# A common issue order for the second batch's attention beside the first batch's mixer, with its levels in single pieces

## The chip, the cores and the metric

One NeuronCore of a Trainium2 chip runs the whole kernel. The metric is the device time of one execution in microseconds (us); lower is better. In this kernel TensorE multiplies matrices (7,828 matmuls in the profile), VectorE (729 instructions) and ScalarE (452) do elementwise work, GpSimd (46) sets masks, and SyncE issues most of the transfers. "Granted clock" is a column of the profile, the share of TensorE's full clock that was granted; the profile records its changes, and in the two profiles compared here its values are 1.00 and 0.50.

## The reference

```python
# r, k, v, w: (4 batches, 8 heads, 768 tokens, 48); u: (8, 48); all float32
for t in range(S):                                   # attention with a running state
    cur = einsum('bhd,bhe->bhde', u[None] * k_t, v_t)
    y[:, :, t] = einsum('bhd,bhde->bhe', r_t, state + cur)
    state = w_t[..., None] * state + einsum('bhd,bhe->bhde', k_t, v_t)
x = y.transpose(0, 2, 1, 3).reshape(4, 768, 384)
h = maximum(x.T_tokens @ w_tok1, 0) @ w_tok2         # mixes tokens (256 hidden)
z = x + h.T
out = z + maximum(z @ w_ch1, 0) @ w_ch2              # mixes channels (1536 hidden)
```

The mixer's weights arrive as 64-bit floats and are turned into 32-bit floats on the chip, in pairs of blocks, by six VectorE instructions and one ScalarE instruction a pair.

## The kernel before

Attention is done in twelve units of 256 tokens, three units a batch. Inside a unit six levels (l = 0 to 5) combine ever larger blocks of tokens (the units of the third and fourth batch combine two levels at a time): each level has a product of keys and queries (`gram`), an in-place scaling of both (`join`) and a copy of the wanted part of the product (`pick`). The first product takes special copies of the queries and keys, `rp` and `kp`, which ScalarE makes. Then the keys are transposed (`tokens`, copied to `kT`), the state's increments are computed (`carry`, to `kv_ps`), the state is advanced (`update`), and the output is the sum of two products (`before` from the state, `within` from the levels) in `y_ps`. One PSUM buffer serves `kv_ps` and `y_ps` in turn.

While one batch's mixer runs, the next batch's attention runs beside it. Two lists of pieces with weights are merged by their share of the total:

```python
def woven(*lists):
    keyed = []
    for n, pieces in enumerate(lists):
        total, at = sum(c for c, _ in pieces), 0.0
        for i, (c, f) in enumerate(pieces):
            keyed.append(((at + c / 2) / total, n, i, c, f))
            at += c
    return [(c, f) for *_, c, f in sorted(keyed, key=lambda e: e[:3])]

def strict(*fs):                  # each engine keeps the order of emission
    for f in fs:
        done = len(block.instructions)
        f()
        for ins in block.instructions[done:]:
            if ins.engine in in_turn:
                tc.add_manual_dep(ins, in_turn[ins.engine], no_sync, reason="order of issue")
                in_turn[ins.engine] = ins.name
```

Outside `strict`, the scheduler of the compiler chooses the order of each engine's instructions. In the kernel before, the stage of the first batch's mixer and the second batch's attention is free in this way; later stages are strict:

```python
        def block(l):
            gram(l); join(l, products[l], products[l + 1]); pick(l)   # one piece of the list
# ... in beside(i, after, ahead), for the second batch's units:
            return [(1.0, begin[1]), tokens, one(carry, rest[0]), update, one(before, rest[1]), one(within, rest[2]),
                    *loads[:2], *rest[3:], ...]
# ... in quarters(s), seven products with ten or so VectorE additions around them:
            if bt == 0:
                return [(0.01, begin)] + [(1.96, p) for p in (p1, p4, p2, p5, p6, p7, p3)]
# ... in the loop over batches:
            if bt == 0:
                emit(woven(att, pieces))                              # free
            else:
                if bt == 1:
                    in_turn = {e.engine: newest(e) for e in (pe, dve, act)}
                strict(*(f for _, f in woven(att, pieces)))
```

## Time and profile before

| | kernel before |
|---|---|
| time, median | 589.5 us (588.8 to 590.2), profiled execution 593.75 |
| span of the profiled execution | 591.4 us |
| TensorE, VectorE, ScalarE busy | 95%, 66%, 30% |
| first stretch (conversions), 94.3 to 127.9 | 33.6 us |
| first mixer + second attention, 127.9 to 226.4 ("the stage") | 98.5 us |
| from there to the end | 365.0 us |

The stage is taken here from the first product of `h_ps` of the channel mixer (line 652) to the first product of the next batch's token mixer (line 615). This is the view of busy time by windows: start and end, length, then busy us and count of TensorE, TensorE's weight loads, VectorE, ScalarE and GpSimd, then granted clock, share of the DMA engines and GB/s.

### The profile page before, as it was taken

The numbers are of one execution on the slowest core, as the hardware profiler recorded it, in microseconds if no ns is written. First come the engines' busy times: TensorE is split into PE (matmuls) and PEld (weight loads), VectorE is DVE, ScalarE is ACT, GpSimd is POOL, SyncE is SP. The second block draws the span as 40 slices with busy tenths as digits, with TensorE's granted clock in tenths as the row PEclk, the third lists the DMA queues.
The fourth block names the chain that finished last, engine by engine and source line by source line (L and its number), as shares of the span: only waits on it lengthen the run. The fifth ranks groups of instructions, "written<-read, shape, count | busy, mean of one in ns | idle before, by whom it ended". The sixth has DMA issues, their size and how long they took to land.

```text
span 591.4 us, 17486 instructions
## 1 busy us (share of the span) xinstructions
PE 562.9 (95%) x7828; PEld 484.6 (82%) x7828; DVE 392.0 (66%) x729; ACT 179.5 (30%) x452; POOL 9.6 (2%) x46
## 2 busy tenths in 40 slices
PE   3779989999999989999999999999999999999997
PEld 2668757876898876789899896889898886898987
DVE  5779699999785696687878775768866232040313
ACT  6144535432414422332323303332313212302020
POOL 4000000000100000000000000000000000000000
PEclk9999999999999999999999999999999999999999
DMA  8526465612224224123232022011010000000000
GB/s 333 211 63 166 133 210 180 200 47 80 76 84 109 71 68 149 28 55 86 77 109 89 23 94 68 1 55 50 7 55 29 1 28 1 0 28 1 27 1 27
DMA packets 23017, 46.13 MB, mean 78 GB/s; under 512 B 2464, under 2 KB 14880, under 8 KB 22944
## 3 DMA queue, kind: packets, MB, share of 16 engines
q1 hardware_dynamic: 22800, 45.03, 24.4%
q8 instruction: 61, 1.00, 0.7%
q14 instruction: 12, 0.10, 0.1%
q10 hardware_dynamic: 144, 0.00, 0.0%
HBM read 40.31 MB, written 4.72 MB: 76 GB/s over the span
## 4 chain that ended last, share of the span: by engine, by line
PE 78%; DVE 13%; issue 3%; DMA 3%; ACT 2%; SPq 0%; DVEq 0%; ACTq 0%
PE z_ps L642 27%; PE q_ps L676 23%; PE gram L308 4%; PE h_ps L622 4%; PE h_ps L615 4%; PE gram L386 3%; PE kv_ps L524 2%; PE y_ps L576 2%; PE h_ps L652 2%; PE gram L513 2%; DVE rk L342 2%; PE y_ps L563 2%; DVE scratch L218 2%; DVE scratch L215 1%; PE gram L302 1%
## 5 line engine op out<-in xcount | busy, mean ns | idle before, releaser
L642 PE MATMUL z_ps<-xT,wch 128*128 128x256 f32 x864 | 194.4, 381 | 1.6 <-ACT z L644 1.6
L642 PEld LDWEIGHTS z_ps<-xT,wch 128*128 128x128 f32 x864 | 161.5, 190 | 24.4 <-ACT z L644 2.6
L644 ACT ACTIVATE z<-z_ps 128x256 f32<-128x256 f32 x144 | 55.0, 383 | 178.0 <-PE z_ps L642 177.9
L676 PE MATMUL q_ps<-wch,z 128*128 128x192 f32 x528 | 93.4, 328 | 0.0
L676 PEld LDWEIGHTS q_ps<-wch,z 128*128 128x128 f32 x528 | 86.5, 190 | 1.3
L676 PE MATMUL q_ps<-scratch,z 128*128 128x192 f32 x396 | 69.6, 328 | 0.0
L676 PEld LDWEIGHTS q_ps<-scratch,z 128*128 128x128 f32 x396 | 64.8, 190 | 0.7 <-issue 0.3
L308 PEld LDWEIGHTS gram<-rk 48*64 48x64 f32 x1536 | 35.3, 177 | 8.9 <-issue 4.0
L308 PE MATMUL gram<-rk 48*64 48x32 f32 x1536 | 37.7, 256 | 5.0 <-issue 2.6
L720 DVE TENSOR_TENSOR z<-z 128x768 f32<-128x768 f32 x9 | 8.6, 954 | 47.4 <-ACT z L644 47.4
L342 DVE TENSOR_TENSOR rk<-rk,decay 112x1024 f32<-112x1024 f32 x24 | 29.4, 1224 | 15.3 <-PE gram L302 9.8
L412 DVE COPY_PREDICATED at<-mask,gram 128x384 f32<-128x384 uint8 (+2 forms) x72 | 34.5, 482 | 1.4
L622 PE MATMUL h_ps<-h,wtok 128*128 128x384 f32 x96 | 35.0, 491 | 0.0
L615 PE MATMUL h_ps<-x,wtok 128*128 128x384 f32 x96 | 34.0, 507 | 0.0
L342 DVE TENSOR_TENSOR rk<-rk,w 112x1024 f32<-112x1024 f32 x24 | 29.3, 1223 | 6.5 <-PE gram L308 6.1
L624 DVE TENSOR_TENSOR x<-x,h_ps 128x384 f32<-128x384 f32 x24 | 13.2, 551 | 30.5 <-PE h_ps L622 30.5
L615 PEld LDWEIGHTS h_ps<-x,wtok 128*128 128x128 f32 x96 | 18.2, 195 | 11.1
L622 PEld LDWEIGHTS h_ps<-h,wtok 128*128 128x128 f32 x96 | 16.5, 190 | 9.8 <-ACT h L617 2.6
L580 ACT COPY x<-y_ps 128x384 f32<-128x384 f32 x12 | 5.8, 479 | 58.4 <-PE y_ps L576 58.4
L686 DVE TENSOR_TENSOR o<-x,z 128x192 f32<-128x192 f32 x11 | 3.9, 356 | 26.3 <-ACT z L685 26.2
L544 DVE TENSOR_TENSOR state<-state,kv_ps 128x192 f32<-128x192 f32 x40 | 14.1, 353 | 9.4 <-PE kv_ps L524 8.1
L285 PE MATMUL gram<-rp,kp 48*64 48x64 f32 x384 | 10.2, 270 | 10.3 <-ACT kp L273 8.1
(114 smaller groups left out, 658.3 us busy)
## 6 DMA issues: line engine op xcount, KB each, us to landing
rk<-in_rkw_dram SPq DMA_DIRECT2D x32, 192.0 KB, 3.7
vt<-in_v_dram SPq DMA_DIRECT2D x12, 384.0 KB, 3.8
out_dram<-o SPq DMA_DIRECT2D x24, 192.0 KB, 1.9
rp<-in_near_dram SPq DMA_DIRECT2D x12, 384.0 KB, 3.6
rk<-in_rkw_dram SPq DMA_DIRECT2D x8, 512.0 KB, 5.6
w<-in_rkw_dram SPq DMA_DIRECT2D x16, 192.0 KB, 3.6
x<-in_w_ch_dram SPq DMA_DIRECT2D x6, 512.0 KB, 4.7
rk<-in_w_ch_dram SPq DMA_DIRECT2D x6, 512.0 KB, 4.3
```

The lines of the kernel that those rows point to most:

```text
L218: dve.scalar_tensor_tensor(mf, mf, 2.0 ** -20, power.bitcast(bf16), op0=ALU.mult, op1=ALU.mult)
L308: fours(lambda q, j, rows, cols: pe.matmul(g[cols, q, ts(ca, 32)], k_[rows, ds(ca * 128 + j * T, T)], right[rows, ts(2 * ca + j, 32 // b), ...
L342: dve.tensor_mul(halves, halves, by)
L386: fours(lambda q, j, rows, cols: pe.matmul(g[cols, q, ts(a, 96)], k_[rows, ds((c * A + a) * 128 + j * T, T)], L["far", c][rows, ts(2 * a + ...
L412: dve.copy_predicated(out=to[:, :, :, (q + 1) * b:], data=got[:, :, :, first * b:first * b + n], mask=masks4[l][:, q].unsqueeze(1).unsquee ...
L544: dve.tensor_add(new, new, got)
L615: pe.matmul(sums[i], wtok1[:, c, ts(i, 128)], xs[bt][:, c, :], start=(c == 0), stop=(c == C - 1))
L622: pe.matmul(ps, wtok2[:, i, ts(c, 128)], h1[:, i, :], start=(i == 0), stop=(i == DTOK // 128 - 1))
L624: dve.tensor_add(x[:, c, :], x[:, c, :], ps)
L642: pe.matmul(ps, wch1[:, m, ts(jt, 128)], xT[:, m, ts(s, SEG)], start=(m == 0), stop=(m == DM // 128 - 1))
L644: act.activation(zs[s][:, jt, :], ps, AF.Relu)
L676: pe.matmul(ps, a[:, j, :], b[:, j, :], start=(j == 0), stop=(j == HJ - 1))
```

## The change

The intent was to give TensorE, VectorE and ScalarE one common order in this stage, as in the later ones, to split the levels into single pieces so that other work can stand between them, and to keep the conversion pairs from overtaking each other. The core of the diff (cuts marked):

```diff
     def whole(steps):
-        return (0.2, lambda: [f() for f in steps])
+        def all_steps():
+            mark = converted[-1]
+            for f in steps:
+                late(mark, dve, f)
+            converted.append(newest(dve))
+        return (0.2, all_steps)
...
+        if i >= UB:
+            pieces = [(0.1, begin), (1.9, lambda: join(0, ...)), (0.3, lambda: [gram0(c) for c in range(UC)]),
+                      *((0.7, lambda c=c: pick0(c)) for c in range(UC))]
+            for l in range(1, LEVELS):
+                pieces += [(0.3, gram l), (1.5, join l), (1.3 if l == 1 else 0.7, pick l)]
+            return pieces
...
-            if bt == 0:
-                return [(0.01, begin)] + [(1.96, p) for p in (p1, p4, p2, p5, p6, p7, p3)]
             return [(1.6, p1), (0.01, <sum s1>), (0.65, p4), ..., (0.3, p6), (1.0, p7), (1.6, p3)]
...
-            return [(1.0, begin[1]), tokens, one(carry, rest[0]), update, one(before, rest[1]), one(within, rest[2]),
-                    *loads[:2], *rest[3:], ...]
+            join0, gram0, pick0, pick1, *rest = rest
+            return [(0.3, tokens[1]), begin, join0, (0.3, both_of(carry, gram0)), loads[2], pick0, loads[3], pick1,
+                    (0.3, both_of(before, rest[0])), *rest[1:3], (0.3, both_of(within, rest[3])), *loads[:2], *rest[4:], ...]
...
-        total = sum(c for c, _ in pieces)              # units of the third and fourth batch
-        return [(c * 12 / total, f) for c, f in pieces]
...
-            if bt == 0:
-                emit(woven(att, pieces))
-            else:
-                if bt == 1:
-                    in_turn = {e.engine: newest(e) for e in (pe, dve, act)}
-                strict(*(f for _, f in woven(att, pieces)))
+            if bt == 0:
+                in_turn = {e.engine: newest(e) for e in (pe, dve, act)}
+            strict(*(f for _, f in woven(att, pieces)))
```

`loads[2]` and `loads[3]` are the two halves of the state update. No instruction is removed; orders change.

More of the change, by code (lines that the diff above doesn't have):

```diff
@@ L420, in levels @@
                 (1.5, join_r, (l,)), (1.5, pick4, (l, 0)), (1.5, pick4, (l, 1)))] + [(1.4, lambda: block(5))]
+        if i >= UB:
+            pieces = [(0.1, begin), (1.9, lambda: join(0, products[0], products[1])), (0.3, lambda: [gram0(c) for c in range(UC)]),
+                      *((0.7, lambda c=c: pick0(c)) for c in range(UC))]
+            for l in range(1, LEVELS):
+                pieces += [(0.3, lambda l=l: gram(l)), (1.5, lambda l=l: join(l, products[l], products[l + 1])),
+                           (1.3 if l == 1 else 0.7, lambda l=l: pick(l))]
+            return pieces
         for l in range(1, LEVELS):
@@ L665, in quarters @@
             L = {}
-            def begin():
-                dve.tensor_add(s1, a21, a22)
-                dve.tensor_sub(s2, s1, a11)
-                dve.tensor_sub(s4, a12, s2)
-                dve.tensor_sub(a21, a11, a21)
             def product(a, b):
@@ L741, in both, with both_of @@
                 tc.add_manual_dep(ins, behind, no_sync, reason="products in tiles together")
-        def one(*pieces):
-            return (sum(c for c, _ in pieces), lambda: both(*(f for _, f in pieces)))
+        def both_of(f, g):
+            return lambda: both(f[1], g[1])
         if i + 1 < NEAR:
-            return [(1.0, begin[1]), tokens, one(carry, rest[0]), update, one(before, rest[1]), one(within, rest[2]),
-                    *loads[:2], *rest[3:], *([(0.0, begin_near)] if i == NEAR - 2 else [])]
+            join0, gram0, pick0, pick1, *rest = rest
+            return [(0.3, tokens[1]), begin, join0, (0.3, both_of(carry, gram0)), loads[2], pick0, loads[3], pick1,
+                    (0.3, both_of(before, rest[0])), *rest[1:3], (0.3, both_of(within, rest[3])), *loads[:2], *rest[4:],
+                    *([(0.0, begin_near)] if i == NEAR - 2 else [])]
         far0, far1, copies, gram, join_k, join_r, pick0, pick1 = rest[:8]
@@ L754, in visit @@
         def visit(f, g):
-            return (0.3, lambda: both(f[1], g[1]))
-        pieces = [*nearest(i), (0.3, tokens[1]), (1.9, begin[1]), far0, far1, (1.0, copies[1]), visit(carry, gram), join_k, join_r, loads[2],
+            return (0.3, both_of(f, g))
+        return [*nearest(i), (0.3, tokens[1]), (1.9, begin[1]), far0, far1, (1.0, copies[1]), visit(carry, gram), join_k, join_r, loads[2],
                   later0, pick0, loads[3], later1, copies_, pick1, visit(before, gram_), join_k_, join_r_, (0.01, lambda: load_near(i + 1)),
                   pick0_, pick1_, visit(within, last), *loads[:2]]
-        total = sum(c for c, _ in pieces)
-        return [(c * 12 / total, f) for c, f in pieces]
     hiddens, turned, ups, downs = mixing(0)
@@ L791, in rwkv6_then_mixer @@
         if bt == 0:
+            converted = [in_turn[dve.engine]]
             to_ch = [whole(e[n < 2:]) for n, e in enumerate(to_ch)]
@@ L797, in rwkv6_then_mixer @@
             weight_sums()
-            converted = newest(dve)
+            summed = newest(dve)
             load_rkw(UB + 2)
@@ L812, in rwkv6_then_mixer @@
             if bt == 0:
-                begin, first, *rest = levels(n)
-                att = [begin, (first[0], lambda f=first[1]: late(in_turn[dve.engine], dve, lambda: late(
-                    in_turn[pe.engine], pe, f)))] + [(c, lambda f=f: late(converted, dve, f)) for c, f in rest]
+                begin, join0, *rest = levels(n)
+                att = [begin, join0] + [(c, lambda f=f: late(summed, dve, f)) for c, f in rest]
             for i in range(n, n + UB):
```

## The prediction

> **What bounds the kernel now.** I first read the busy time by stage (window start and end, length, then busy us and instruction count of each engine), because TensorE's 95% over the span hides stages of different kinds.
>
> ```profile
> 94.30:128.00 33.70, 32.13 (x150) 27.50 (x149) 31.93 (x40) 16.62 (x32) 0.00 (x0) 1.00 0.51 157
> 139.60:154.00 14.40, 14.31 (x410) 11.18 (x411) 13.08 (x20) 5.42 (x15) 0.00 (x0) 1.00 0.09 31
> 154.00:173.00 19.00, 18.98 (x520) 17.62 (x510) 15.36 (x28) 6.00 (x15) 2.50 (x15) 1.00 0.35 96
> 173.00:202.00 29.00, 28.64 (x751) 24.37 (x744) 17.98 (x33) 11.25 (x30) 0.11 (x1) 1.00 0.32 85
> 202.00:226.50 24.50, 22.64 (x524) 20.85 (x522) 23.02 (x59) 6.41 (x19) 0.11 (x1) 1.00 0.34 92
> 226.50:356.00 129.50, 129.50 (x1678) 113.55 (x1678) 96.29 (x204) 36.48 (x101) 0.23 (x2) 1.00 0.25 75
> ```
>
> From 139.6 to 226.5 the mixer of batch 0 runs beside the attention of batch 1: this is the stage the change reorders. TensorE idles there only 2.3 us (differences of the first two columns), and from 226.5 on not at all. So whatever the stage gains or loses, the end gains or loses. VectorE is nearly full in its first and last windows.
>
> Then the timeline, for the waits a new order can lengthen.
>
> ```profile
> 140.81 0.66 ACT L269 COPY kp<-rk 112x512 f32<-112x512 f32 x1 [12.35 <-PE gram L285]
> 141.37 1.31 ACT L273 ACTIVATE kp<-rk,u_col 112x128 f32<-112x128 f32 x4
> 142.58 0.67 ACT L269 COPY rp<-rk 112x512 f32<-112x512 f32 x1
> 142.71 1.23 DVE L342 TENSOR_TENSOR rk<-rk,w 112x1024 f32<-112x1024 f32 x1
> 143.14 1.32 ACT L273 ACTIVATE rp<-rk,u_col 112x128 f32<-112x128 f32 x4
> ...
> 160.38 0.67 ACT L269 COPY kp<-rk 112x512 f32<-112x512 f32 x1 [2.33 <-issue]
> 160.96 1.31 ACT L273 ACTIVATE kp<-rk,u_col 112x128 f32<-112x128 f32 x4
> ...
> 183.98 1.13 PE L285 MATMUL gram<-rp,kp 48*64 48x64 f32 x64
> ```
>
> ScalarE makes kp and rp in 1.87 us each (140.81 to 142.68), 3.75 us a unit (a unit is 256 tokens). The first product of keys and queries (line 285) needs both. The first in-place scaling of rk (line 342) may start only when kp has read rk: it starts at 142.71, just after the last of kp. At present the third unit's kp is ready 22 us before its product.
>
> ```profile
> 172.25 1.02 PEld L308 LDWEIGHTS gram<-rk 48*64 48x64 f32 x64 [0.23 <-DVE rk L342]
> 173.46 1.23 DVE L342 TENSOR_TENSOR rk<-rk,decay 112x1024 f32<-112x1024 f32 x1 [0.43 <-PE gram L308]
> ...
> 187.77 0.35 DVE L544 TENSOR_TENSOR state<-state,kv_ps 128x192 f32<-128x192 f32 x1
> 188.26 1.15 PE L563 MATMUL y_ps<-state,rk 48*64 48x48 f32 x64 [0.36 <-DVE state L544]
> ```
>
> Two more loops. A level's product starts 1.21 us before its scaling can (172.25 to 173.46), and scaling to the next level's product took 1.28 to 1.36 us (147.12 to 148.40, 149.60 to 150.96): about 2.5 us a level, of which the product fills 1.07, so some 1.4 us of other TensorE work must lie between. And y_ps takes the only buffer of its kind from kv_ps, so it waits for the last state update (line 544).
>
> [...]line 308's loads keep PEld busy 1.02 us a visit while waits of 0.23 to 0.55 us around visits hardly show in PE.[...]
>
> **The change, part by part.**
>
> *Conversion pairs one by one.* No operation is removed, but VectorE can no longer take a later pair's first step early. Two lines show what that costs now:
>
> ```profile
> 117.21 0.69 DVE L210 TENSOR_SCALAR scratch<-scratch 128x1024 uint16<-128x1024 uint16 x1 [1.15 <-DMA scratch<-in_w_ch_dram]
> 122.59 5.45 PE L642 MATMUL z_ps<-xT,wch 128*128 128x256 f32 x24 [0.85 <-ACT z L644]
> ```
>
> Three attention steps leave this stretch too (1.15+0.65+0.65). A pair is 0.61+0.61+1.26+1.26+1.27 = 5.0 us, so the ninth ends near 129.2 instead of 133.2. But TensorE gains little: its 24 z_ps tiles of six recorded matmuls (1.30 us) start near 96 either way, behind the additions of h_ps, and each pair's line 211 on ScalarE still blocks the z copies behind it until VectorE reaches that pair. Laying the pairs beside the tiles I find two stalls, about 1.0 and 0.5 us, for about 2 now, and a start perhaps 0.4 later: tiles end at 127.9 instead of 128.0. Gain 0 to 1; I take 0.3.
>
> *The stage, in strict order.* I took the new order of each engine from the built kernel and laid it out by hand with the durations above and these from the timeline, in us: h_ps and z_ps pieces 1.30, a q_ps product 1.95, line 302 0.68, transposes 0.9, kT copies 1.07, late copies into at 1.5, scaling 1.15 plus its product 0.2 to 0.65, picks 0.67 to 1.3, state pair 0.78, quarter sums 0.87 each. Time t runs from the first of the last four h_ps pieces (138.3 now). TensorE waits where the order forces it:
> - First unit: 0.6 for the first pick (only two gram buffers, and the second level now follows at once). Before the third scaling VectorE must add an h_ps that TensorE finishes only at 7.8; the scaling runs 8.45 to 9.6, the product starts at 9.75: 2.0. Level 5: 0.8. Small ones 0.3.
> - Second unit: rp and kp now come on ScalarE after the first unit's kT, which wait for its transposes (19.65): kT until 20.85, rp and kp until 24.6. TensorE has only one q_ps product and kv_ps between, to 22.7; its product ends at 25.3 for 0.93 of work: 1.6. VectorE's scaling also waits to 24.7, and then 9.45 us of VectorE work stand before kv_ps is free (34.15): scaling and its product 1.8, four additions to the output 0.36+0.5+0.76+0.88, two quarter sums 1.74, a pick 0.67, seven state operations 2.74. Meanwhile TensorE has three q_ps, to 31.25: 3.0. Levels 4 and 5 stand together without filler: 1.6. Small ones 0.3.
> - Third unit: kT come behind a 1.5 us copy: 0.95. Then rp and kp to 55.7: 2.4. Then 5.6 us of VectorE work (1.8, a pick 0.67, four state pairs' worth 3.1) until y_ps may start at 61.5, with one z_ps (to 57.7) for filler: 3.8. Levels with 1.30 of filler: 3 times 0.15.
> - Last part: kT 1.05, copies for the next unit 0.5, q_ps buffer 0.55, second gram buffer 1.35.
>
> The sum is 3.7+6.5+7.6+3.45 = 21.3, and the stage ends at t = 102.9 instead of 226.4-138.3 = 88.1: **+14.8**. So the work itself is 102.9-21.3 = 81.6 in this layout, and the present stage holds 6.5 us of waits and tile switches.[...]
>
> *Weights of the weave.* For the third batch's stage the common scaling to 12 is gone, so its last unit is squeezed into the last sixth. There six state operations stand before the seventh product's addition: 2.35+0.95 us from the sixth product, against 1.95 of TensorE: +1.4. The stage of the second batch keeps its order; the last has no attention.
>
> Sum: 589.5 - 0.3 + 14.8 + 1.4 = 605.4. I shade it to 604, since my layout charges every wait in full and VectorE may regain some.
>
> **Rivals.**
> - *It works as meant.* Fewer visits, quarter sums spread out, the 2.3 us idle gone, conversions 4 us shorter on VectorE: at best 2.3+0.6+2 less, 585. For it: the later stages already run in strict order without a gap. Against: those units need no rp and kp products, which make the long ScalarE chain here.
> - *The stalls are absorbed.* If VectorE ran far enough ahead, only the waits of ScalarE's chain would stay (1.6+0.95+2.4), +5 with the rest: 594. Against: the 9.45 us and 5.6 us of VectorE work start only when that chain ends, so they can't run ahead.
> - *Worse.* [...]the conversion's line 211 stalls more tiles: +3, 608; a late state pushes waits into the next stage as well: 611.
>
> **Range and chances.** The second and third unit's waits (14.1 of the 21.3) rest on two measured dependencies and I trust them to 3 us; the rest to another 3. That gives 597 to 610. Slower by over 2% begins at 601.3. Since the stage can't give more than 5 us, faster by 2% (577.7) is nearly excluded: 0.02. Same 0.28, slower 0.70.
>
> **What would show it.** TensorE idle 10 to 20 us between the h_ps pieces and the next batch's line 615; waits of line 285 on ScalarE's kp, twice, near 2 us; of y_ps on the state update, twice, 3 to 4; ScalarE's rp and kp directly behind kT; tiles of the conversion stretch ending within 1 us of 128; no idle in the following stage. It is wrong if line 285 finds kp ready, or y_ps finds its buffer free, or if the stages after 226 change by more than 2.

## More of the kernel before

```profile
127.88:226.41 98.53, 96.19 (x2201) 80.59 (x2200) 80.93 (x150) 29.38 (x79) 2.72 (x17) 1.00 0.29 82
356.06:482.76 126.70, 126.50 (x1494) 110.66 (x1487) 83.32 (x172) 35.76 (x95) 0.00 (x0) 1.00 0.10 32
482.76:591.40 108.64, 105.40 (x536) 92.58 (x534) 24.92 (x46) 18.53 (x47) 0.00 (x0) 1.00 0.04 13
```

In the stage TensorE is idle for 98.53 - 96.19 = 2.34 us and its clock is full throughout.

## The result

The changed kernel took 611.5 us (median of four executions, 609.2 to 614.2) against 589.2 us of the kernel before in the same runs. The ratio is 1.038, with a 95% interval of 1.033 to 1.043. Ratios here are the mean time of one kernel's fast runs over that of the other's of the same rounds, so they are not quite the ratio of the medians quoted. The prediction, 604 with a range of 597 to 610, had the direction right and missed by 7.5 us; the result lies 1.5 us above the range.

The two profiles start this stage 3.9 us apart (127.9 and 124.0). That is no merit of the change: of the later runs with the same early code some start it near 124 and some near 128. So stages are compared by their lengths. The same view for the changed kernel:

```profile
90.34:124.00 33.66, 32.17 (x150) 27.39 (x148) 32.65 (x40) 17.55 (x35) 0.00 (x0) 1.00 0.47 150
124.00:242.35 118.35, 103.91 (x2202) 86.28 (x2200) 80.69 (x146) 32.85 (x93) 2.34 (x17) 0.94 0.23 65
242.35:371.98 129.63, 129.63 (x1686) 113.70 (x1678) 98.74 (x209) 35.98 (x101) 0.22 (x2) 1.00 0.26 78
371.98:500.29 128.31, 126.87 (x1494) 110.23 (x1487) 84.02 (x173) 34.04 (x92) 0.00 (x0) 1.00 0.10 32
500.29:609.10 108.81, 105.50 (x540) 92.73 (x534) 24.55 (x45) 19.91 (x50) 0.00 (x0) 1.00 0.04 13
```

The first stretch is as long as before (33.66 against 33.59), the stage is 19.8 us longer, the following one is unchanged, the third batch's is 1.6 longer. Inside the stage idle time grew from 2.34 to 118.35 - 103.91 = 14.44 us, that is by 12.1; and the *same 2,200 products* kept TensorE busy 7.7 us longer. The mean granted clock of 0.94 would explain most of that: a lost share of 6% of 118 us is by estimate about 7 us.

The waits of TensorE in the stage, summed by what waited and what ended the wait (total us, times, longest):

```profile
PE y_ps L577 <- DVE state L558: 5.7, 2, 3.2
PE gram L292 <- ACT kp L280: 2.3, 2, 1.5
PE gram L315 <- DVE rk L349: 1.9, 1, 1.9
PE gram L309 <- DVE rk L349: 1.3, 1, 1.3
```

These four groups are 11.2 of the 14.44 us, and they are the loops that the prediction named. One of them in order of time (start, duration, engine, line, operation, and in brackets the idle time before it with its releaser):

```profile
187.84 1.07 ACT L529 COPY kT<-gram 128x512 f32<-128x512 f32 x2
188.80 0.72 ACT L276 COPY rp<-rk 112x512 f32<-112x512 f32 x1
189.35 0.76 ACT L276 COPY kp<-rk 112x512 f32<-112x512 f32 x1
191.11 1.37 ACT L280 ACTIVATE kp<-rk,u_col 112x128 f32<-112x128 f32 x4
191.64 1.70 PE L292 MATMUL gram<-rp,kp 48*64 48x64 f32 x64 [1.52 <-ACT kp L280]
192.51 1.23 DVE L349 TENSOR_TENSOR rk<-rk,w 112x1024 f32<-112x1024 f32 x1 [6.61 <-ACT kp L280]
...
197.53 0.35 DVE L558 TENSOR_TENSOR state<-state,kv_ps 128x192 f32<-128x192 f32 x1
198.03 1.96 PE L577 MATMUL y_ps<-state,rk 48*64 48x48 f32 x64 [3.20 <-DVE state L558]
```

ScalarE makes `rp` and `kp` only after `kT`, because the common order says so. TensorE waits 1.52 us for `kp`; VectorE stands 6.61 us before it may scale the keys, then does scaling, state updates and picks in a row, and TensorE waits 3.20 us for the last state. The first unit's loop at the third scaling is there too:

```profile
142.55 0.56 DVE L670 TENSOR_TENSOR o<-x,h_ps 128x384 f32<-128x384 f32 x1 [1.25 <-PE h_ps L666]
143.03 1.22 DVE L349 TENSOR_TENSOR rk<-rk,w 112x1024 f32<-112x1024 f32 x1
144.39 1.14 PE L315 MATMUL gram<-rk 48*64 48x32 f32 x64 [1.87 <-DVE rk L349]
```

The conversion stretch has two short waits of tiles of `z_ps` for ScalarE's copies, 1.2 us in all (1.6 before). The longer one:

```profile
122.60 1.56 PE L656 MATMUL z_ps<-xT,wch 128*128 128x256 f32 x6 [0.80 <-ACT z L658]
```

What I had not predicted is in the durations. The `y_ps` product of 198.03 took 1.96 us for 64 matmuls, the same that took 1.15 in the profile before (303 ns against 218 for the median matmul). Six windows of the changed kernel, in the form of the view by windows:

```profile
142.85:146.26 3.41, 1.87 (x67) 1.59 (x68) 2.90 (x5) 0.00 (x0) 0.00 (x0) 1.00 0.16 58
146.26:149.67 3.41, 3.41 (x68) 2.27 (x67) 2.68 (x5) 0.10 (x1) 0.00 (x0) 0.50 0.17 58
149.67:153.09 3.42, 3.42 (x11) 3.42 (x12) 1.66 (x3) 1.34 (x4) 0.00 (x0) 0.50 0.24 58
...
194.05:197.46 3.41, 0.79 (x4) 0.36 (x2) 3.17 (x9) 0.38 (x1) 0.00 (x0) 1.00 0.41 115
197.46:200.87 3.41, 2.84 (x108) 2.87 (x109) 1.03 (x3) 0.16 (x1) 0.11 (x1) 0.50 0.00 0
200.87:204.29 3.42, 3.42 (x38) 2.51 (x33) 2.56 (x3) 0.00 (x0) 0.00 (x0) 0.50 0.45 120
```

After a window in which TensorE was busy only 1.87 or 0.79 of 3.41 us, its clock was 0.50 for exactly two windows. The edges were found by reading the clock in steps of half a microsecond: falls from 146.26 to 153.09 and from 197.46 to 204.29, 6.83 us each. As an estimate from the recorded 0.50, 13.66 us at half clock lose up to 6.8 us of product time; TensorE was busy for 13.1 of them, which makes it 6.5. (Products measured there took 1.7 to 1.8 times as long: 1.96 us against 1.15 for `y_ps`, and 2.87 us at 201.60 against 1.56 at 193.27 for six recorded matmuls of `z_ps`.)

Not every long wait was followed by a fall. The wait of 2.47 us that ended at 171.13 lies in two windows, the first of which still had 1.92 us of work, and the clock stayed full:

```profile
166.74:170.15 3.41, 1.92 (x12) 1.62 (x10) 3.18 (x8) 0.00 (x0) 0.00 (x0) 1.00 0.00 0
170.15:173.57 3.42, 2.44 (x115) 2.40 (x116) 1.83 (x5) 0.16 (x1) 2.12 (x15) 1.00 0.32 85
```

The recorded values in this profile are 1.00 and 0.50 alone. The edges of both falls lie on one grid: each fall is 6.83 us long, and the second begins 51.20 us after the first (197.46 - 146.26), which is 15 times half of 6.83, that is 3.413 us. Falls of that half length were seen alone in later runs (445.82 to 449.24 in e4, 171.6 to 175.0 in e11). The windows above are cut on this grid.

### The profile page after: what moved, and what is told of

Same layout as the page of the kernel before. It is cut to its first block, busy times and chain, and to the rows that moved or that the text cites.

```text
span 609.1 us, 17498 instructions
## 1 busy us (share of the span) xinstructions
PE 569.6 (94%) x7828; PEld 489.5 (80%) x7828; DVE 394.9 (65%) x729; ACT 177.8 (29%) x452; POOL 9.2 (2%) x46
## 4 chain that ended last, share of the span: by engine, by line
PE 74%; DVE 16%; issue 3%; ACT 3%; DMA 2%; SPq 0%; DVEq 0%; ACTq 0%
PE z_ps L656 26%; PE q_ps L684 23%; PE gram L315 4%; PE h_ps L636 4%; PE h_ps L629 4%; PE h_ps L666 3%; PE gram L393 3%; DVE scratch L218 2%; DVE scratch L215 2%; DVE rk L349 2%; PE y_ps L590 2%; PE y_ps L577 1%; PE gram L527 1%; PE kv_ps L538 1%; DVE state L558 1%
## 5 line engine op out<-in xcount | busy, mean ns | idle before, releaser
L656 PE MATMUL z_ps<-xT,wch 128*128 128x256 f32 x864 | 197.2, 384 | 1.2 <-ACT z L658 1.2
L684 PEld LDWEIGHTS q_ps<-wch,z 128*128 128x128 f32 x528 | 88.3, 193 | 0.8
L315 PEld LDWEIGHTS gram<-rk 48*64 48x64 f32 x1536 | 36.7, 185 | 11.5 <-issue 4.9
L315 PE MATMUL gram<-rk 48*64 48x32 f32 x1536 | 39.0, 262 | 6.9 <-issue 2.2
L726 DVE TENSOR_TENSOR z<-z 128x768 f32<-128x768 f32 x11 | 10.5, 955 | 47.4 <-ACT z L658 47.4
L638 DVE TENSOR_TENSOR x<-x,h_ps 128x384 f32<-128x384 f32 x24 | 13.2, 550 | 29.3 <-PE h_ps L636 29.3
L629 PEld LDWEIGHTS h_ps<-x,wtok 128*128 128x128 f32 x96 | 18.1, 195 | 11.2
L577 PEld LDWEIGHTS y_ps<-state,rk 48*64 48x64 f32 x704 | 14.6, 156 | 12.3 <-issue 9.2
L577 PE MATMUL y_ps<-state,rk 48*64 48x48 f32 x704 | 16.2, 242 | 7.5 <-DVE state L558 7.5
L292 PE MATMUL gram<-rp,kp 48*64 48x64 f32 x384 | 11.4, 274 | 12.5 <-ACT kp L280 10.3
L339 ACT COPY at<-gram 16x256 f32<-16x256 f32 x24 | 8.7, 362 | 43.5 <-PE gram L315 42.6
```

Source lines behind the costliest of these rows:

```text
L315: fours(lambda q, j, rows, cols: pe.matmul(g[cols, q, ts(ca, 32)], k_[rows, ds(ca * 128 + j * T, T)], right[rows, ts(2 * ca + j, 32 // b), ...
L577: pe.matmul(y[put(q, j), q, ds((c * A + a) * D, D)], r_[q * P:q * P + D, ds((c * A + a) * 128 + j * T, T)], state[bt, g][q * P:q * P + D, ...
L629: pe.matmul(sums[i], wtok1[:, c, ts(i, 128)], xs[bt][:, c, :], start=(c == 0), stop=(c == C - 1))
L638: dve.tensor_add(x[:, c, :], x[:, c, :], ps)
L656: pe.matmul(ps, wch1[:, m, ts(jt, 128)], xT[:, m, ts(s, SEG)], start=(m == 0), stop=(m == DM // 128 - 1))
L684: pe.matmul(ps, a[:, j, :], b[:, j, :], start=(j == 0), stop=(j == HJ - 1))
```

## The experiments

After this result my theory was: the common order puts `kp` and the state late, TensorE waits, and the waits additionally trip the half clock. Rivals were: the conversions; the third batch's weights; the levels' split and the quarters' weights; and falls of the clock that have nothing to do with waits. Twelve kernels ran. All gave correct results. The kernel before had medians of 589.9 (beside e1 to e4), 591.2 (e5 to e8), 590.3 (e9 to e11) and 589.4 us (e12), so ratios are compared across calls.

The first table holds the stage of every profiled execution: its length, TensorE's idle time (length less busy), and the time lost to half clock (an estimate: half of the length at 0.50).

| kernel | median us | ratio | stage | idle | lost to clock |
|---|---|---|---|---|---|
| before | 589.2 | 1 | 98.5 | 2.3 | 0 |
| changed | 611.5 | 1.038 | 118.4 | 14.4 | 6.8 |
| e1 conversions only | 589.0 | 0.999 | 98.4 | 2.3 | 0 |
| e2 third batch's weights | 611.5 | 1.036 | 117.2 | 13.2 | 6.8 |
| e3 kp early | 605.0 | 1.025 | 113.1 | 10.3 | 6.8 |
| e5 kp and state early | 601.7 | 1.018 | 106.9 | 7.2 | 3.4 |
| e6 three orders | 595.1 | 1.007 | 101.3 | 5.1 | 0 |
| e7 quarters only | 595.0 | 1.008 | 101.3 | 4.9 | 0 |
| e8 ScalarE free | 605.1 | 1.024 | 111.5 | 10.0 | 5.1 |
| e9 true weights | 619.0 | 1.050 | 124.6 | 17.6 | 10.2 |
| e10 even | 601.2 | 1.020 | 109.2 | 8.8 | 5.1 |
| e11 third scaling first | 609.5 | 1.033 | 115.9 | 11.2 | 8.5 |
| e12 shifted filler | 592.2 | 1.006 | 100.6 | 4.1 | 0 |

In each row the stage is idle + clock loss + 95.3 to 97.3 us (96.2 before). So these two terms account, within about 1 us, for what the orders cost in this stage. Where much of a stage is at half clock, the two are not independent: at half clock a product takes longer (1.96 us against 1.15 for `y_ps`) and may fill part of a wait, and idle time at half clock is counted in both.

### e1: the conversions alone

```diff
 # kernel before
-        return (0.2, lambda: [f() for f in steps])
+        def all_steps():                      # as in the change: each pair behind the pair before
+            mark = marks[-1]
+            for f in steps: late(mark, dve, f)
+            marks.append(newest(dve))
```

> The kernel before with only the conversion pairs put strictly one by one. My theory: hardly any effect, 588.3 to 589.3 us against 589.2 (I predicted a gain of 0.3). Rival A: the new order starves ScalarE's copies of z_ps, +1.5 or more, 590.7 or above. Rival B: the head start of about 3.4 us that the profile of the changed kernel shows at 80 us comes from the conversions, so the time is about 585.8.

Measured: 588.96 against 589.92 us, ratio 0.9988 (0.9975 to 1.0001). The conversions cost nothing and perhaps gain 0.7 us; the first stretch is 32.83 us here against 33.59. Rivals A and B both fall. It is the only run whose median is below the kernel before, and its interval touches 1.

A caution on mean clocks: this profile (mean clock 0.988) reads 1.00 in the first stretch and in the stage, so an estimated 14 us at half clock (0.012 x 586.8 / 0.5) lie outside them; in e7 and e8 half clock was recorded from 54 to 71 and from 52 to 69 us, before this stretch too. The profile of the kernel before (mean clock 1.000) has no recorded change of the clock until 72.75 us, and reads 1.00 there; yet a matmul of `y_ps` (L563) took 303 ns at 65 to 70 us, as it does under the recorded 0.50 at 198.03 in the changed kernel (303 ns), and 218 ns at 75 to 80. So a mean of 1.000 does not mean that the clock was never halved, and the mean clocks of executions can't be compared as if it did.

### e2: the third batch's old weights

```diff
 # changed kernel
-        return [*nearest(i), ...]
+        pieces = [*nearest(i), ...]
+        total = sum(c for c, _ in pieces) if i >= NEAR else 12
+        return [(c * 12 / total, f) for c, f in pieces]
```

> The changed kernel with the common scaling to 12 put back for the far units alone, which gives the third batch's stage its old order. My theory: that stage had lost 1.4 to 1.7 us, so 609.8 to 610.1 against 611.5. Rival: the loss after 242 us comes from something else (a late end of the stage before), and the time stays within 0.5 of 611.5.

Measured: 611.51 us (607.8 to 612.5), the same median as the changed kernel. By the time alone the rival wins. The trace shows more:

```profile
374.80:501.49 126.69, 126.49 (x1495) 110.66 (x1487) 83.32 (x172) 35.74 (x95) 0.00 (x0) 1.00 0.10 32
```

The third batch's stage is back at 126.69 us, against 128.31 in the changed kernel and 126.70 before. So the weights cost 1.6 us there, which the scatter of the stage before it (executions 5 us apart) hides in the total.

### e3: kp and rp early on ScalarE

```diff
 # changed kernel, second batch's units
-            return [tokens, begin, join0, (carry, gram0), update_0, pick0, update_1, pick1, (before, gram1), ...
+            return [tokens, join0, (carry, gram0), update_0, pick0, update_1, pick1, <begin of the next unit>, (before, gram1), ...
```

> The changed kernel with ScalarE making rp and kp of the next unit right behind the previous unit's first pick, 20 us sooner; no other engine's order changes. My theory: the two waits on kp (0.74 and 1.52 us) go, the first scaling of the second and third unit starts earlier, so the waits of y_ps on the state update (2.47 and 3.20) shrink below 1 each, and without a long wait at 190 to 198 the second fall of TensorE's clock (about 3.2 us) goes too: 601 to 603 us, one fall left. Rival A, the level order without filler is the main cause and VectorE's own work takes the place of the waits: 607 to 609. Rival B, the falls of the clock have nothing to do with the waits: two falls remain, 604 to 606.

Measured: 605.0 us, ratio 1.025. The waits on `kp` are gone and the first scaling of the second unit starts at 156.35 instead of 161.78, but one `y_ps` wait stayed:

```profile
162.21 0.56 DVE L706 TENSOR_TENSOR o<-x,q_ps 128x384 f32<-128x384 f32 x1 [2.90 <-PE q_ps L684]
...
168.56 1.14 PE L577 MATMUL y_ps<-state,rk 48*64 48x48 f32 x42 [2.48 <-DVE state L558]
```

VectorE is now early, yet it stands idle for 2.90 us before an addition of the mixer that the order puts ahead of the state update. The state is late by order, not by load. Idle time fell by 4.1 us; the clock still fell, for about four windows of 3.41 us by the stage's mean clock of 0.94. My 601 to 603 was too low because this wait and the clock stayed; 605.0 is in rival B's range.

### e4: forced waits in a stage without any

```diff
 # kernel before, second and third batch's stages: before every fourth z_ps product
+                pe.matmul(ps[:, :8], pause[:, :128], pause[:, :8], start=True, stop=True)
+                for _ in range(n):            # n = 2 to 9
+                    pool.memset(pause, 0.0)
+                pe.matmul(ps[:, :8], pause[:, :128], pause[:, :8], start=True, stop=True)
```

> The kernel before with 18 forced waits of TensorE in the second and third batch's stages, where it is never idle: between two tiny products GpSimd writes their operand 2 to 9 times in a row, by an estimate 1.4 to 5 us of wait, 57 us in all. My theory, that waits of 2 us and more can halve TensorE's clock for 6.4 us: the 13 waits with four writes and more are followed by a granted clock of 0.50, at 3.2 us each 42 us more, about 688 us with a mean clock near 0.94. Rival, the falls are no matter of waits: clock 1.00, 646 us. A threshold between shows as the shortest wait with a fall behind it.

Measured: 682.1 us, mean clocks 0.941 to 0.954 (0.949 in the profile). In the profile the 18 waits sum to 55.1 us (two writes made one of 1.28 us, eight one of 4.77), and 13 of them are followed by half clock, eight for one window of 3.41 us and five for two: 61.4 us at half clock, by the same estimate 30.7 us lost. That sums to 590 + 55 + 31 = 676; 6 us are left unexplained. The rival's 646 at full clock falls. All ten waits of five and more writes were followed by half clock in this profile, two of three with four writes, none of three with three, and one of the two with two writes. Here are windows on this run's grid (edges at 254.68 and every 3.413 us), for waits of eight and of four writes and for one of five:

```profile
254.68:258.09 3.41, 0.14 (x3) 0.05 (x1) 0.45 (x3) 0.39 (x1) 2.85 (x6) 1.00 0.01 2
258.09:261.50 3.41, 1.90 (x6) 1.64 (x7) 0.00 (x0) 0.00 (x0) 1.34 (x3) 0.50 0.00 0
261.50:264.92 3.42, 3.42 (x10) 2.70 (x9) 0.00 (x0) 0.38 (x1) 0.00 (x0) 0.50 0.00 0
264.92:268.33 3.41, 3.41 (x104) 2.95 (x106) 0.00 (x0) 1.84 (x7) 0.00 (x0) 1.00 0.02 5
425.34:428.75 3.41, 1.90 (x10) 1.72 (x11) 3.27 (x10) 0.07 (x1) 1.34 (x3) 1.00 0.02 5
428.75:432.17 3.42, 3.42 (x18) 3.01 (x17) 3.25 (x9) 1.08 (x3) 0.00 (x0) 1.00 0.00 0
442.41:445.82 3.41, 0.48 (x3) 0.48 (x4) 2.79 (x8) 0.21 (x1) 2.62 (x5) 1.00 0.68 231
445.82:449.24 3.42, 3.42 (x9) 2.68 (x9) 0.00 (x0) 0.38 (x1) 0.00 (x0) 0.50 0.00 0
449.24:452.65 3.41, 3.41 (x60) 3.07 (x63) 0.20 (x1) 0.70 (x2) 0.00 (x0) 1.00 0.00 0
```

A window with 0.14 or 0.48 us of work was followed by a half-clock window; one with 1.90 us (425.34) was not. These figures give no bound: another window of this run with 2.13 us (244.44 to 247.85, with the wait of 1.28 us) was followed by half clock. The same wait was followed by a fall in one execution and not in the next: the second unit's `y_ps` wait was 2.47 us with no fall in the changed kernel's profile, 2.48 us with a fall in e3 and 2.47 us with a fall in e8. The grid lay elsewhere in those runs whose edges were read: from 146.26 in the changed kernel it is 31.8 steps to 254.68 in e4 and 6.5 to 168.43 in e8. That a wait is shared between two windows in one execution (1.92 and 2.44 us busy in the changed kernel) and lies within one in another (165.64 to 168.11 in e8, in the window before 168.43) is my reading of the difference.

### e5: the state updates first

```diff
 # on top of e3
-            (carry, gram0), update_0, pick0, update_1, pick1,
+            (carry, gram0), (0.01, update_0), (0.01, update_1), (2.1, pick0), (2.1, pick1),
```

> As e3, and VectorE's state updates of a unit directly behind its product kv_ps, ahead of the quarter's additions and of the picks; TensorE's order unchanged. In e3 y_ps still waited 2.48 and 0.96 us for the state. My theory: the first wait goes, the second falls to about 0.3, and the two half-clock windows behind the 2.48 us wait (169 to 176 in e3, 3.4 us lost) go as well: 605.0 - 2.4 - 0.7 - 3.4 = 598.5. Rival A, the waits matter but the clock falls elsewhere instead: 602. Rival B, VectorE is the bound there and the wait moves to a pick or a scaling: 604 to 605.

Measured: 601.7 us, ratio 1.018. The waits were as expected: the second unit's `y_ps` starts without one, the third waits 0.47. In the profiled execution (600.06 us) the stage is 6.2 us shorter than in e3: idle time is 3.2 less and the clock loss 3.4 less, nearly the sum of my theory. The windows at half clock are not quite those that I expected, though: the one behind the first unit's wait (145 to 149) stayed as in e3, the one at 196 went too, and one came behind a wait of 1.35 us of a fifth level (179 to 183). By the median, Rival A's 602 is the better number.

### e6: the third scaling before the addition

```diff
 # on top of e5
+            k = turns.index(<third h_ps piece of the stage>)
+            turns[k:k + 2] = turns[k + 1], turns[k]      # third scaling of the first unit goes first
-            pieces = downs[0][-4:] + [weight_difference] + downs[1] + ...
+            pieces = downs[0][-4:] + downs[1][:3] + [weight_difference] + downs[1][3:] + ...
```

> As e5, and in the first unit the third scaling ahead of the addition of h_ps on VectorE (with the product of h_ps behind the scaling's turn), and the weight difference three quarter steps later. My theory: the wait of 1.87 us and the half-clock window that followed it in all three profiles go, so 1.9 + 1.7 to 3.4 less, and 0.4 at the fifth level: 594.0 to 595.5. Rival A, no clock effect: 2.2 less than e5. Rival B: the addition of h_ps, now later, keeps its buffer and h_ps waits instead: no more than 1 less than e5.

Measured: 595.1 us (594.0 to 597.7), ratio 1.007.

```profile
123.91:225.18 101.27, 96.20 (x2202) 80.47 (x2200) 80.52 (x145) 33.14 (x93) 2.98 (x17) 1.00 0.26 76
```

The profiled execution has full clock in the stage, and TensorE's busy time is 96.20 us against 96.19 before, with the same number of products. Four moves in the order (`rp` and `kp`, the state, the third scaling, the weight difference), no instruction less, took 16.4 us off the changed kernel. This is the strongest evidence that late order, waits and the clock behind them are the cause.

### e7: only the quarters' sums and weights

```diff
 # kernel before
-            if bt == 0:
-                return [(0.01, begin)] + [(1.96, p) for p in (p1, p4, p2, p5, p6, p7, p3)]
```

> The kernel before with only the quarters' sums spread over the seven products and their weights changed as in the change; no strict order, no split levels. My theory: this part is not what costs, 588.5 to 590.5. Rival: the later sums leave the products of sums waiting for VectorE, 592 or more.

Measured: 595.0 us, ratio 1.008, outside my range; the rival's number was right. Its mechanism was hardly seen: no product waits for a sum, and two `q_ps` products wait 0.6 and 0.4 us for VectorE to free their buffers. The stage is 2.8 us longer, with 2.5 us more of idle time: small waits of levels, quarters and one state. That the weights of 0.3 to 1.6 for products of equal length bunch the filler is my reading; this run changes sums and weights together. The rest, 1.0 us by the medians and 1.7 by the ratio, I could not place; the part after the stage is unchanged at 365.0.

### e8: ScalarE left to the scheduler

```diff
 # changed kernel, second batch's stage
-                in_turn = {e.engine: newest(e) for e in (pe, dve, act)}
+                in_turn = {e.engine: newest(e) for e in (pe, dve)}
```

> The changed kernel with the strict order in the second batch's attention for TensorE and VectorE only; ScalarE's order is left to the scheduler, which then puts rp and kp of the second and third unit before the last level's copies of the first or right after its kT. My theory: near e3, since only kp's lateness counts on ScalarE: 604 to 606.5. Rival, ScalarE's strict order has other good or bad effects (copies of z_ps, of the last levels): 608 or more, or below 603.

Measured: 605.1 us, ratio 1.024, as expected and as e3: no wait on `kp` is left. So `kp` is about all that ScalarE's strict order cost, 6.4 us of the 22 by the medians.

### e9: the quarters' true weights

```diff
 # changed kernel, quarters of the first batch
-            return [(1.6, p1), ..., (0.65, p4), ..., (0.65, p2), ..., (0.45, p5), ..., (0.3, p6), (1.0, p7), (1.6, p3)]
+            return [(1.96, p1), ..., (1.96, p4), ..., (1.96, p2), ..., (1.96, p5), ..., (1.96, p6), (1.96, p7), (1.96, p3)]
```

> The changed kernel with each quarter product of the second batch's stage weighted by its true 1.96 instead of 0.3 to 1.6, so that TensorE's filler is spread evenly over the attention; kp and the states stay late. In e7 the low weights alone cost the kernel before about 2.8 us in its stage. My theory: filler moves from the first unit's end to the levels of the second and third, so 1.3 at a fifth level goes, but the kp chain gets a product less in front: net 1 to 3 less, 608.5 to 610.5. Rival, the low weights are the main cause of the stage's loss and not the order on ScalarE and VectorE: 603 or less.

Measured: 619.0 us, ratio 1.050. Both theories fall. I expected a gain from even filler, since e7 had shown the opposite move to cost; under strict order it is the worst of all. The waits of its stage:

```profile
PE y_ps L577 <- DVE state L558: 6.0, 3, 3.1
PE gram L315 <- DVE rk L349: 5.2, 3, 2.0
```

With true weights the second quarter's sums and additions come earlier and stand among the third unit's work, where a new `y_ps` wait of 3.06 us arises, and two more levels wait. A weight moves VectorE's instructions as well as TensorE's; in strict order that decides.

### e10: everything mended at once

```diff
 # e6 + e9 + e2, and:
+   third scaling ahead of the last h_ps product; p5 ahead of kv_ps; first z_ps product ahead of gram(4)
```

> All mendings together: e6 with the true weights of e9, three hand-made swaps (the third scaling ahead of the last h_ps product, the fifth quarter product between transposes and kv_ps, the first z_ps product ahead of the fourth level's), and the third batch's old weights of e2. My theory, from e6's remaining waits (1.35 fifth level, 1.2 kT, 0.5 y_ps) and 1.65 of the third batch: 595.1 - 4.7 = 590.4 beside 591.2 of the kernel before in the same runs, without a fall of the clock. Rival, the strict order itself costs more than the before kernel's free scheduler whatever the pieces: 593 or more.

Measured: 601.2 us, ratio 1.020: the rival, and worse than e6. The expected waits went, but the new one of e9 is there:

```profile
223.79 0.35 DVE L558 TENSOR_TENSOR state<-state,kv_ps 128x192 f32<-128x192 f32 x1
224.29 1.15 PE L577 MATMUL y_ps<-state,rk 48*64 48x48 f32 x64 [3.06 <-DVE state L558]
```

From 215 to 224 VectorE has no idle time in this run: the state of the third unit comes after two further quarter sums of 0.95 us each. The clock fell for two windows directly after.

### e11: only the first unit

```diff
 # changed kernel: the two edits of e6 without those of e3 and e5
```

> The changed kernel with only the first unit mended: the third scaling ahead of the addition of h_ps on VectorE, and the weight difference later. My theory: the wait of 1.87 us goes, 0.4 at the fifth level, and the one or two half-clock windows that follow it (1.7 or 3.4): 606.0 to 607.8. Rival, the clock falls all the same: 609.3.

Measured: 609.5 us (607.9 to 612.8), ratio 1.033, the rival's number. The wait of 1.87 us and the fall behind it are gone, but in the profiled execution the remaining waits were followed by five windows at half clock instead of two: half clock at 171.6 to 175.0, 185.2 to 188.6 and 195.5 to 205.7. So mending one wait does not buy back "its" fall reliably; that the number of falls is a matter of how the grid meets all waits is my reading.

### e12: filler one slot earlier

```diff
 # on top of e6, with e2's weights
+   ten z_ps products of the stage one slot earlier (one before each level of the second and third unit)
+   copies of level 5 directly behind their product
```

> As e6, with ten z_ps products of the second batch's stage one slot earlier, so that one stands before each level of the second and third unit, the last level's copies on ScalarE directly behind their product, and the third batch's old weights of e2; the quarters keep the low weights (e10 failed with the true ones). My theory, from e6's waits: 1.35 at the fifth level and 1.2 at kT go, and 1.65 in the third batch: 595.1 - 4.2 = 590.9 where the kernel before has 590 to 591, no fall of the clock. Rival, as in e10 new waits take their place: 594 or more.

Measured: 592.2 us (591.4 to 599.6) against 589.4, ratio 1.006 (1.003 to 1.009). The waits I aimed at went (idle 4.1 us), a new one of 1.24 us on a quarter's addition came. It is the best of the strict orders and still 0.6% behind the kernel before; none of the runs beats the kernel before by a clear margin.

## Why the prediction was wrong in size

**Conversions, gain 0.3.** The changed kernel has 33.66 us there against 33.59, so no gain; alone (e1) 0.7. Right within half a microsecond.

**Stage, +14.8: measured +19.8.** The sum had two sides. The waits, 21.3 less the 6.5 that the layout charged to the present, became 14.44 less 2.34, so +12.1 for +14.8. That these are so close is partly luck: the layout charged 6.9 us too much for waits, and 4.2 too much to the present stage (it spoke of waits and tile switches; TensorE was idle for 2.34, and no trace here shows what a switch costs). The longer waits that it named were found, and each was shorter (the 0.8 of the first unit's fifth level did not appear; the product before it ran at half clock):

| wait | predicted | measured |
|---|---|---|
| first unit, third scaling | 2.0 | 1.87 |
| second unit, kp / y_ps | 1.6 / 3.0 | 0.74 / 2.47 |
| second unit, levels without filler | 1.6 | 1.34 |
| third unit, kT / kp / y_ps | 0.95 / 2.4 / 3.8 | 0.64 / 1.52 / 3.20 |
| last part, second gram buffer | 1.35 | 0.99 |

**The step that failed** is "the work itself is 102.9-21.3 = 81.6 in this layout": it took every product at the duration of the profile before, where the clock was 1.00 throughout the stage. The work is no constant. After waits of 1.9 and 3.2 us the clock was 0.50 for 6.83 us each time, and the same products took 103.9 instead of 96.2 us. By estimate 6.5 to 6.8 of these 7.7 us are the missing term (in e4, 13 of 18 forced waits were followed by half clock; in e6, without the long waits, the stage's clock was 1.00). Idle time gives +12.1 and the clock +6.5 to +6.8; about 1 us more of busy time, for which no cause was looked for, completes the 19.8. "I shade it to 604, since my layout charges every wait in full" was fair for the waits and pushed the total the wrong way.

**Weave, +1.4:** measured +1.6, and e2 takes it back. The stages after 226 changed by 1.75 us in all, inside the 2 that the prediction allowed.

**Rivals.** "It works as meant" failed for the reason given, ScalarE's long chain (e3, e8); its 0.6 for fewer visits was an estimate that no trace shows. "The stalls are absorbed" failed as argued: the state could not run ahead. "Worse, 611" had the number but not the reason: no wait was pushed into the next stage (129.63 us, no idle). The range was set from the error of waits alone; no part of it allowed for the clock.

**Two small slips.** "From 226.5 on not at all" is not so: TensorE is idle there for 0.2 us in the third batch's stage and 3.2 in the last. And the sign "tiles of the conversion stretch ending within 1 us of 128" failed by the clock (124.0), because this execution had reached the stretch 4 us sooner; the stretch itself was as long as before.

**What stays open.** What about a window decides is not settled by the busy time shown here (in e4 1.90 us passed, 2.13 fell). The scatter of the changed kernel's executions (609.2 to 614.2) fits a varying number of windows, an estimated 1.7 us each (half of 3.41), but only profiled executions show where they lie. The split of the levels was never run alone; e12, which keeps it, is 0.6% behind the kernel before. Why e7 costs 1 to 1.7 us more than its stage shows is open, and so are the 6 us in e4.

## What to carry to other kernels

When an order is laid out by hand, ask of each engine what the new order puts ahead of the one instruction that another engine waits for; here a few such moves were worth 16 of 22 us. A TensorE stall of about 2 us in a stage that is otherwise full may cost more than the wait: here such stalls were followed by none, one or two windows of 3.41 us at half clock (three once, in e11), half of which I count as lost, by estimate. Piece weights move every engine's instructions, so check VectorE's queue after changing TensorE's filler.

## What the traces show of the clock

- Waits of these lengths were followed by falls here: 1.87 us (window with 1.87 of 3.41 us busy) and 3.20 us (0.79 us busy) in the changed kernel, and a forced wait of 1.28 us in e4 (2.13 us busy). The wait's length alone does not decide: 2.47 us, shared by two windows with 1.92 and 2.44 us busy, was followed by none in the changed kernel.
- Nor does the busy time of the window, as measured: 2.13 us was followed by a fall in e4, 1.90 us there and 1.92 us in the changed kernel were not.
- In most cases a fall lasted one window of 3.41 us (eight of thirteen in e4, four of five in e9's stage). But after 146.26 in the changed kernel a window with TensorE busy throughout, by the profile's busy time, was followed by a second half-clock window; so it was in e8 (from 168.43), and in e3 the fall behind the wait of 2.48 us lasted two windows as well (169 to 176). Of the three in a row of e11 (195.47 to 205.71) the first two had 2.10 and 2.51 us busy.
